# A gather kernel on one Trainium2 core: each gather waits for the landing of the fourth gather ahead of it

## The chip, the cores and the metric

The kernel runs on one core of a Trainium2 chip. A core has a matrix engine (PE, with its weight loads shown as PEld), a vector engine (DVE), a scalar engine (ACT), GpSimd (POOL) and SyncE (SP), each with its own queue of instructions that it works off in order, and 16 DMA engines that they share. The metric is the device time of one execution in microseconds (us); lower is better. Every time comes from the runs or from one profiled execution.

## The reference

Two parts are added to the input `x` (2048 rows of 448), both fed by its layer norm `xn`. The first is a long convolution per channel. The second, a mixture of 4096 experts, is where the change lies: for each row and each of 16 heads, two experts are chosen, their rows of `u` and `v` are fetched, and their outputs are summed. In the code below, `k_shift` is a causal convolution of `k` with four taps, `y` one of `kv` with `ssm_k` over the whole length, done with an FFT; `top_s` and `top_e` are the two best of the four sums made from the two best of `s1` and of `s2`.

```python
def _A_ref(q, k, v, shift_k, ssm_k, ssm_D):
    ...
    kv = k_shift * v
    ...
    return q * (y + kv * ssm_D)

def _B_ref(x, w_q, k1, k2, u, v):
    q = jnp.einsum("nd,dhc->nhc", xf, w_q)
    s1 = jnp.einsum("nhd,ed->nhe", q[..., :dk], k1)
    s2 = jnp.einsum("nhd,ed->nhe", q[..., dk:], k2)
    ...
    g = _softmax(top_s, axis=-1)
    ue = u[top_e]
    ve = v[top_e]
    act = _gelu(jnp.einsum("nd,nhkd->nhk", xf, ue))
    return jnp.einsum("nhk,nhk,nhkd->nd", g, act, ve)

xn = _layernorm(x, axis=-1)
return x + _A_ref(xn, A_k, A_v, A_shift_k, A_ssm_k, A_ssm_D) + _B_ref(xn, B_w_q, B_k1, B_k2, B_u, B_v)
```

## The kernel before

The 2048 rows are 16 tiles (`T`) of 128. For each tile there are 128 x 32 chosen experts, and they are worked on in blocks (`b`, 128 in all, eight per tile). A block is four gathers: one indirect DMA of POOL (L494) takes 128 indices from `idx` and fetches 128 rows of `uv`, the expert's `u` and `v` side by side, 896 float32 each. The four gathers of a block fill one buffer `uv`, and there are four buffers (`NBUF`, the pool `gp`), so POOL can be at most four blocks ahead of the reader that frees a buffer.

A block is then read as follows. `e_spread` (L506) spreads the normed rows into `xr` on PE. `e_dots` multiplies the `u` halves by `xr` on DVE: L525 takes the first `na` of the four gathers in one instruction and leaves their sums to ACT (L544), and L532 takes each of the rest with its sum. ACT applies gelu (L548), DVE weighs by the gate (L559), the weights are spread into `cc`, and PE (L584 and L587) multiplies the `v` halves by `cc` into `pv`. That last matmul frees the buffer: in the code it is the key `("v", b)`, for which the first gather of block b + 4 waits.

The convolution runs in two halves (`g`) beside this, in the second half of the time. `c_load` (L624) brings seven blocks of its inputs from `hkv` with SP's DMAs into `x1`, shown in the profile as `x`; `c_delta` (L660) and `c_prod` on DVE read them first. `c_fm` (L697) brings the tables `fm`, 66 of 128 KB, for its matmuls.

The order of all engines is fixed before the program runs. Each stage is a generator of operations with an assumed cost; a planner (`Planner`) starts them one by one on a model of the engines and writes the instructions out in that order. Waits on the chip come from the dependences between instructions: the tile framework adds semaphore waits where an instruction reads or overwrites what another makes. DMAs of POOL take eight semaphores (`DMASW0` to `DMASW7`) in turn.

Of the kernel before, what the change touches and what calls it, by code (L numbers as in the profile page):

```python
# [185 lines left out]
def parallel_kernel(ctx, tc, x, wq, kk, uv, hkv, const, fq, out):  # L186
    nc = tc.nc
    ctx.enter_context(tc.manual_schedule())
    ap = ctx.enter_context(tc.tile_pool(name="ap", bufs=1))
# [21 lines left out]
    idx = ap.tile([P, NT, NG], I32, name="idx")  # L211
# [14 lines left out]
    live = {}  # L226
# [258 lines left out]
    NB = len(order)  # L485
    HALF = CH * GC

    def e_gather():
        for b, (T, j, hf) in enumerate(order):
            for c in range(4):  # L490
                def go(b=b, T=T, g=8 * j + 4 * hf + c, c=c):
                    if c == 0:
                        live["uv", b] = gp.tile([P, 4, 2 * D], F32, tag="uv", name="uv")
                    nc.gpsimd.indirect_dma_start(live["uv", b][:, c, :], None, uv, bass.IndirectOffsetOnAxis(ap=idx[:, T, g:g + 1], axis=0))  # L494
                yield Op("POOL", 1.25, go, [("idx", T)], key=("land", b, c), moved=4.6e5, rings=[(r_uv, ("v", b))] if c == 0 else [])

    def e_spread():
# [310 lines left out]
    plan.add(2, norm(6, NT))  # L808
    plan.show("weights")
    experts = [plan.add(PRIO.get(s.__name__, 0.0), s()) for s in (e_gather, e_values, e_weigh, e_scale, e_spread, e_dots, e_gelu, e_out, e_fold)]  # L810
    stores = [plan.add(1, e_store(g)) for g in range(2)]
    plan.run(early)
# [72 lines left out]
```

## Time and profile before

| | |
|---|---|
| runs | 998.83, 1013.42 and 1013.01 us, median 1013.01 |
| profiled execution | 1002.79 us |
| its span, first to last instruction | 1001.0 us |
| granted PE clock, mean | 0.853 of full speed |
| DMA | 278.52 MB, mean 278 GB/s over the span |

A group's row in the profile gives line, engine, operation, `output<-inputs`, the form and the count, then busy time in us, mean ns of one, and the idle time of the engine just before these instructions with what ended it. "issue" is waiting for which the profile shows no cause. A wait for several semaphores is put down to the one that came last. In a timeline, each row has start, duration and, in brackets, the idle time before it and who ended that.

### The profile page before, as it was taken

The page shows a single profiled execution, that of the slowest core. Times are in us where ns is not written, and L with a number is a line of the kernel's source. Part 1 is how long each engine was busy: PE and PEld are TensorE (multiplying, and loading weights), DVE is VectorE, ACT ScalarE, POOL GpSimd, SP SyncE. Part 2 cuts the span into 40 slices and gives each one's busy share as a digit, 9 for nine tenths or more (in the row PEclk, how much of TensorE's full clock was granted, in tenths as well). Part 3 has the DMA queues.
Part 4 walks back from the last instruction along what each step waited for, and adds up shares of the span by engine and source line. Part 5 has one row for each costly group of instructions (what it writes and reads, how often), then busy time and mean ns, then how long its engine had stood idle before and what let it go on. Part 6 is the DMA issues. An engine that isn't in the chain of part 4 may idle for free.

```text
span 1001.0 us, 16542 instructions
## 1 busy us (share of the span) xinstructions
PE 741.3 (74%) x5052; PEld 422.7 (42%) x5052; DVE 711.1 (71%) x2621; ACT 543.6 (54%) x1886; POOL 491.5 (49%) x518
## 2 busy tenths in 40 slices
PE   6971889697988878765576777776767665778775
PEld 3550446454454545333443333444444422333443
DVE  3575989698887778773677768873666857789444
ACT  4313786366756566464565546563276554556532
POOL 0024463556655455655465455554355655555450
PEclk9995789898999788865779889997887897899777
DMA  9936785778887787889988688989788878899674
GB/s 343 381 117 234 246 287 192 267 252 300 297 278 267 252 280 251 297 275 378 330 283 266 235 309 274 351 286 381 255 286 277 288 257 295 308 311 329 239 231 148
DMA packets 80553, 278.52 MB, mean 278 GB/s; under 512 B 10320, under 2 KB 47568, under 8 KB 80464
## 3 DMA queue, kind: packets, MB, share of 16 engines
q0 software_dynamic: 40960, 234.91, 67.9%
q1 hardware_dynamic: 39360, 42.41, 12.6%
q8 instruction: 41, 0.67, 0.3%
q10 hardware_dynamic: 144, 0.13, 0.1%
q14 instruction: 48, 0.39, 0.1%
HBM read 273.75 MB, written 3.67 MB: 277 GB/s over the span
## 4 chain that ended last, share of the span: by engine, by line
PE 39%; DVE 23%; issue 11%; ACT 9%; another core or an unknown queue 8%; DMA 7%; POOL 2%; DVEq 0%; SPq 0%; POOLq 0%; ACTq 0%
DVE uv L525 8%; PE pv L587 7%; ACT uv L544 5%; DVE mi L397 5%; PE ps L677 4%; PE psf L705 4%; PE fin L773 4%; DVE mx L399 3%; DMA x<-in_hkv_dram 3%; PE pw L296 3%; PE psu L737 3%; DMA uv<-in_uv_dram,idx 3%; PE sc L355 2%; POOL uv L494 2%
## 5 line engine op out<-in xcount | busy, mean ns | idle before, releaser
L494 POOL DMA_INDIRECT uv<-in_uv_dram,idx x512 | 490.8, 959 | 485.5 <-issue 154.1
L544 ACT ACTIVATE uv<-uv 128x448 f32<-128x448 f32 x459 | 258.9, 568 | 63.4 <-DVE uv L525 38.9
L525 DVE TENSOR_TENSOR uv<-xr,uv 128x1792 f32<-128x1792 f32 (+3 forms) x128 | 233.0, 1822 | 33.4 <-remote 10.4
L587 PE MATMUL pv<-uv,cc 128*32 128x448 f32 x1024 | 154.9, 637 | 0.2 <-issue 0.2
L677 PE MATMUL ps<-cst,x 128*64 128x132 f32 x896 | 80.4, 336 | 45.0 <-issue 16.9
L397 DVE FIND_INDEX8 mi<-mx,sc 128x8 uint32<-128x64 f32 x512 | 104.3, 221 | 6.3 <-issue 6.2
L705 PE MATMUL psf<-x,fm 128*128 128x448 f32 x132 | 74.1, 656 | 36.4 <-DVE hh L728 18.2
L677 PEld LDWEIGHTS ps<-cst,x 128*64 128x64 f32 x896 | 63.9, 168 | 78.7 <-issue 36.8
L399 DVE MAX8 mx<-sc 128x8 f32<-128x64 f32 x512 | 74.1, 214 | 31.1 <-remote 15.8
L355 PE MATMUL sc<-wh,xh 128*128 128x512 f32 x192 | 86.1, 448 | 8.2 <-remote 3.7
L544 ACT ACTIVATION_READ_ACCUMULATOR uv<-uv 128x1 f32 x459 | 87.8, 191 | 0.0
L357 PE MATMUL sc<-wh,xl 128*128 128x512 f32 x192 | 79.4, 413 | 1.1 <-issue 1.1
L356 PE MATMUL sc<-wl,xh 128*128 128x512 f32 x192 | 79.7, 415 | 0.3 <-issue 0.3
L737 PE MATMUL psu<-hh,fm 128*128 128x224 f32 x264 | 67.2, 385 | 16.4 <-remote 5.9
L737 PEld LDWEIGHTS psu<-hh,fm 128*128 128x128 f32 x264 | 52.8, 207 | 47.6 <-issue 30.3
L687 ACT ACTIVATE x<-ps 128x396 f32<-128x396 f32 (+1 forms) x84 | 37.3, 459 | 54.0 <-PE ps L677 35.0
L773 PE MATMUL fin<-cst,zt 128*64 128x64 f32 x896 | 49.5, 259 | 22.5 <-issue 22.0
L574 ACT ACTIVATE cc<-rep,w 128x32 f32<-128x32 f32 x212 | 50.2, 311 | 27.3 <-DVE w L559 17.5
L713 ACT ACTIVATE hh<-psf 128x224 f32<-128x224 f32 x66 | 23.2, 354 | 72.2 <-remote 29.8
L355 PEld LDWEIGHTS sc<-wh,xh 128*128 128x128 f32 x192 | 39.4, 205 | 44.2 <-issue 21.3
L584 PE MATMUL pv<-uv,cc 128*1 128x4 bf16 x128 | 21.6, 169 | 49.3 <-ACT cc L574 19.1
L559 DVE TENSOR_TENSOR w<-ge,gt 128x4 f32<-128x4 f32 x128 | 19.9, 156 | 52.1 <-ACT ge L548 35.1
(98 smaller groups left out, 1057.1 us busy)
## 6 DMA issues: line engine op xcount, KB each, us to landing
wq<-in_wq_dram SPq DMA_DIRECT2D x16, 896.0 KB
x<-in_hkv_dram SPq DMA_DIRECT2D x14, 780.0 KB
fm<-in_fq_dram SPq DMA_DIRECT2D x66, 128.0 KB
uv<-in_uv_dram,idx POOLq DMA_INDIRECT x512
out_dram<-acc SPq DMA_DIRECT2D x32, 112.0 KB
acc<-in_x_dram SPq DMA_DIRECT2D x1, 2240.0 KB
acc<-in_x_dram SPq DMA_DIRECT2D x1, 896.0 KB
cst<-in_const_dram SPq DMA_DIRECT2D x1, 540.0 KB
```

The source lines that it names most:

```text
L355: nc.tensor.matmul(sc, xh[:, c, :], wh[:, c, ns], start=(c == 0), stop=False)
L356: nc.tensor.matmul(sc, xh[:, c, :], wl[:, c, ns], start=False, stop=False)
L397: nc.vector.max_index(mi[:, T % 2, 8 * n + j, :], m, sc[:, 64 * j:64 * j + 64])
L399: nc.vector.max(m, sc[:, 64 * j:64 * j + 64])
L494: nc.gpsimd.indirect_dma_start(live["uv", b][:, c, :], None, uv, bass.IndirectOffsetOnAxis(ap=idx[:, T, g:g + 1], axis=0))
L525: nc.vector.tensor_mul(u, live["xr", T, j][:, None, :D].broadcast_to([P, na, D]), u)
L544: nc.scalar.activation(u, u, AF.Copy, accum_out=live["act", b][:, c:c + 1])
L587: nc.tensor.matmul(pv[32 * c:32 * c + 32, :D], cc[:, c, :], buf[:, c, D:], start=(hf == 0), stop=(hf == 1), tile_position=(0, 32 * c))
L677: nc.tensor.matmul(ps[64 * i:64 * i + 64, w * j:w * j + w], src, f1[:, i, :], start=True, stop=True, tile_position=(0, 64 * i))
L705: nc.tensor.matmul(ps[:, :2 * HALF], live["fm", g, q][:, 0], x1[:, :, :, q, :].rearrange("p c t k -> p t c k"), start=True, stop=True)
L737: nc.tensor.matmul(ps[:, :HALF], fm[:, 1], hh[:, i], start=(i == 0), stop=(i == 1))
L773: nc.tensor.matmul(o[64 * n:64 * n + 64], zt[:, j, 64 * ri:64 * ri + 64], f3[:, ri, n, :], start=(ri == 0), stop=(ri == 1), tile_position= ...
```

## The change

The list `sent` keeps every gather's instruction. From the fifth on, a gather gets a synchronising dependence on the gather four before it in the list, that is, on the same place `c` of the block before. Nothing else in the kernel is altered, and the planner doesn't know of the added dependence, so its order is that of before.

```diff
+    sent = []
+
     def e_gather():
         for b, (T, j, hf) in enumerate(order):
             for c in range(4):
                 def go(b=b, T=T, g=8 * j + 4 * hf + c, c=c):
                     if c == 0:
                         live["uv", b] = gp.tile([P, 4, 2 * D], F32, tag="uv", name="uv")
-                    nc.gpsimd.indirect_dma_start(live["uv", b][:, c, :], None, uv, bass.IndirectOffsetOnAxis(ap=idx[:, T, g:g + 1], axis=0))
+                    made = nc.gpsimd.indirect_dma_start(live["uv", b][:, c, :], None, uv, bass.IndirectOffsetOnAxis(ap=idx[:, T, g:g + 1], axis=0)).ins
+
+                    sent.append(made)
+                    if len(sent) > 4:
+                        tc.add_manual_dep(made, sent[-5].name, mybir.DependencyInfo(mybir.DependencyClass.Sync, mybir.DependencyReason.DATA), reason="pace")
```

On POOL, from the first gather on, the instructions before stand as follows. `DMAHW` are the semaphores of loads by SP or ACT, `DMASW` those of the gathers; the n-th gather raises number n - 1 modulo 8 when it has landed.

```order
L494 DMA uv<-in_uv_dram,idx 128x896 [waits DMAHW3_49,DMAHW2_49,Activation_49]
L494 DMA uv<-in_uv_dram,idx 128x896 x3
L494 DMA uv<-in_uv_dram,idx 128x896 [waits DMAHW5_49,DMAHW4_49,PE_49]
L494 DMA uv<-in_uv_dram,idx 128x896 x3
L494 DMA uv<-in_uv_dram,idx 128x896 [waits DMAHW6_49,DMAHW7_49,DMASW0_49,PE_49]
L494 DMA uv<-in_uv_dram,idx 128x896 [waits DMASW1_49]
L494 DMA uv<-in_uv_dram,idx 128x896 [waits DMASW2_49]
L494 DMA uv<-in_uv_dram,idx 128x896 [waits DMASW3_49]
L494 DMA uv<-in_uv_dram,idx 128x896 [waits DMAHW0_49,DMAHW1_49,DMASW4_49,PE_49]
```

There the first wait on `DMASW0` is the ninth gather's, so a gather waits for the eighth ahead of it. With the change, on the same engine from the same place:

```order
L496 DMA uv<-in_uv_dram,idx 128x896 [waits DMAHW3_49,DMAHW2_49,Activation_49]
L496 DMA uv<-in_uv_dram,idx 128x896 x3
L496 DMA uv<-in_uv_dram,idx 128x896 [waits DMAHW4_49,DMAHW5_49,DMASW0_49,PE_49]
L496 DMA uv<-in_uv_dram,idx 128x896 [waits DMASW1_49]
L496 DMA uv<-in_uv_dram,idx 128x896 [waits DMASW2_49]
L496 DMA uv<-in_uv_dram,idx 128x896 [waits DMASW3_49]
L496 DMA uv<-in_uv_dram,idx 128x896 [waits DMAHW6_49,DMAHW7_49,DMASW4_49,PE_49]
```

Now the fifth gather waits on `DMASW0`, the first gather's, and the ninth on `DMASW4`, the fifth's. The gathers themselves stand in the same places.

## The prediction

> **What bounds the kernel now.** The first view is the page's list of engines, with the group of the gathers and that of their first reader.
>
> ```profile
> PE 741.3 (74%) x5052; PEld 422.7 (42%) x5052; DVE 711.1 (71%) x2621; ACT 543.6 (54%) x1886; POOL 491.5 (49%) x518
> ...
> q0 software_dynamic: 40960, 234.91, 67.9%
> ...
> PE 39%; DVE 23%; issue 11%; ACT 9%; another core or an unknown queue 8%; DMA 7%; POOL 2%; DVEq 0%; SPq 0%; POOLq 0%; ACTq 0%
> ...
> L494 POOL DMA_INDIRECT uv<-in_uv_dram,idx x512 | 490.8, 959 | 485.5 <-issue 154.1
> ...
> L525 DVE TENSOR_TENSOR uv<-xr,uv 128x1792 f32<-128x1792 f32 (+3 forms) x128 | 233.0, 1822 | 33.4 <-remote 10.4
> ```
>
> No engine is full. In the chain that ended last (the row of shares), PE and DVE hold 62% and POOL 2%. POOL is idle for 485.5 us, and since it does nothing in the span but the 512 gathers, that is the time it already spends waiting. They are the queue q0 (packets, MB, share of the 16 DMA engines): one gather is 234.91 MB / 512 = 459 kB. What POOL waits for, and who waits for the gathers, stands in the list of waits:
>
> ```profile
> POOL uv L494 <- issue: 154.1, 393, 9.3
> ...
> POOL uv L494 <- ACT uv L544: 54.0, 17, 8.3
> ...
> POOL uv L494 <- PE pv L587: 44.3, 18, 5.5
> ...
> DVE x L660 <- DMA x<-in_hkv_dram: 12.8, 3, 8.0
> ...
> DVE uv L525 <- DMA uv<-in_uv_dram,idx: 7.0, 7, 3.9
> ...
> PE pv L584 <- DMA uv<-in_uv_dram,idx: 2.6, 1, 2.6
> ...
> ACT uv L544 <- DMA uv<-in_uv_dram,idx: 2.1, 1, 2.1
> ```
>
> The columns are total us, times, longest. POOL's waits are for buffers: PE (L587) is a buffer's last reader. The other way round, an engine waited for a gather's landing 9 times, 11.7 us in all. So the gathers run ahead of their readers nearly everywhere, and the readers set the pace. The pace is on POOL's timeline:
>
> ```profile
> 66.48 1.10 POOL L494 DMA_INDIRECT uv<-in_uv_dram,idx  x1 [65.17 <-ACT gt L462]
> ...
> 71.63 0.94 POOL L494 DMA_INDIRECT uv<-in_uv_dram,idx  x1 [0.30 <-issue]
> 72.88 0.95 POOL L494 DMA_INDIRECT uv<-in_uv_dram,idx  x1 [0.30 <-issue]
> ...
> 307.98 0.95 POOL L494 DMA_INDIRECT uv<-in_uv_dram,idx  x1 [0.30 <-issue]
> 313.20 0.94 POOL L494 DMA_INDIRECT uv<-in_uv_dram,idx  x1 [4.28 <-PE pv L587]
> ...
> 972.99 0.95 POOL L494 DMA_INDIRECT uv<-in_uv_dram,idx  x1 [0.30 <-issue]
> ...
> 976.74 0.95 POOL L494 DMA_INDIRECT uv<-in_uv_dram,idx  x1 [0.30 <-issue]
> ```
>
> Inside a buffer's four gathers one starts every 1.25 us (71.63 to 72.88). Over the run it is (976.74 - 66.48) / 511 = 1.78 us, because the first gather of a buffer usually stands still until the buffer is free (4.28 us at 313.20). Only 33 of the 127 later buffers start with no such pause; the first of those is the row at 71.63, the last that at 972.99.
>
> **The change, part by part.** It adds no instruction and moves none. Each gather from the fifth on gets a wait on the landing of the gather four ahead. In the order of POOL nearly every gather already waits on one of eight DMA semaphores, that of the gather eight ahead; the names of the waits stay and only the gather that is meant moves, from eight ahead to four. The first four waits are new: fifth to eighth gather.
>
> What is one such wait worth? It needs the time from a gather's start to its landing. The chain in order of time shows that whole where a reader did wait:
>
> ```profile
> 128.12 4.81 DMA uv<-in_uv_dram,idx
> ...
> 257.17 5.80 DMA uv<-in_uv_dram,idx
> ...
> 513.37 4.44 DMA uv<-in_uv_dram,idx
> ...
> 591.13 4.83 DMA uv<-in_uv_dram,idx
> ...
> 910.22 6.25 DMA uv<-in_uv_dram,idx
> ```
>
> 4.44 to 6.25 us, mean 5.23. The gather four ahead started 4 x 1.25 = 5.0 us earlier if nothing paused, and over 6 us earlier if the buffer's first gather paused by 1.3 us or more. POOL then needs a moment from release to start. A PE release bounds it:
>
> ```profile
> 311.39 1.54 PE L587 MATMUL pv<-uv,cc 128*32 128x448 f32 x8
> ```
>
> The matmul ends at 311.39 + 1.54 = 312.93 and the gather starts at 313.20: 0.27 us. Could a release by a landing take longer? The nearest row is this one, of the same engine, so I take 0.27; zero is the lower end.
>
> So the new wait costs nothing behind a pause: 5.23 + 0.27 = 5.50 us have gone by already. In an unbroken run it costs 5.50 - 5.00 = 0.50 us (none by the shortest landing, 6.25 + 0.27 - 5.00 = 1.52 by the longest), once per run, since the three gathers after it follow landings that are themselves about a gather apart. With 33 unbroken starts that is 33 x 0.50 = 17 us more of waiting on POOL, at most 33 x 1.52 = 50, set against 485.5 us of idle time.
>
> Of that the end sees little. Behind the waiting gather stand only later gathers, for POOL has no other work, and behind those the readers at L525. What hides the delay is the lead of the landings over the readers; if it goes, DVE is late, then ACT (L544) and PE (L587), then the buffer's release. The 9 exposed waits are where there is no lead. A share of 33 / 127 of them, 2.3, follows an unbroken start: 2.3 x 0.50 = 1.2 us. Were all nine hit at the longest landing, it would be 9 x 1.52 = 13.7 us. Below nothing it can go too: a gather that stands back leaves the DMA engines to the loads of L624, for which DVE waited 12.8 us (row above), so -12.8 us is that end. Between -12.8 and +13.7 I take +1, by the exposed waits, since they are the rows of the very thing that is delayed.
>
> The Trainium skill (DMA: Bandwidth & Descriptors, section Anatomy of one DMA — SWDGE (gpsimd) path) gives one DMA from GpSimd about 2.0 us plus its bytes at 436 GB/s, which for 459 kB is an estimated 3.05 us. By that the wait would never bind, 3.05 being under 5.0, and the sum would be 0 instead of +1. The trace disagrees, with 4.44 to 6.25 us under this kernel's load.
>
> **The sum.** The profiled execution took 1002.8 us (span 1001.0); +1 gives 1004. It stands 1% below the median of the three runs shown, 1013.0, whose lowest is 998.8 and highest 1013.4. I put the forecast between the two, at 1007: the change moves nothing by as much as the runs differ among themselves.
>
> **The rivals.**
>
> *The four-deep loop becomes the bound (slower).* With four in flight a gather can start no oftener than every (landing + release) / 4. At 5.50 us that is 1.38 us, and 1.78 is needed, so there is room. It decides from 4 x 1.78 = 7.1 us on; each 0.1 us above then costs 512 x 0.1 / 4 = 12.8 us. For it speaks the 6.25 row, that landings could lengthen where the loads of L624 compete (below), and that a release by a landing is nowhere shown on POOL. Against it: four of the five landings are under 6, and fewer gathers in flight are no reason for one to land later. At 7.3 us it gives 1003 + 26 = 1029 us. A stage alone doesn't reach it: it must hold through the run.
>
> *The loads of L624 come through sooner (faster).* At 449 us seven loads of 0.8 MB start, beside the gathers, and the chain in order of time waits for the third of them:
>
> ```profile
> 449.17 28.77 DMA x<-in_hkv_dram
> ```
>
> The DMA queues in the window from 453 to 466 us:
>
> ```profile
> q0 software_dynamic: 734, 4.24, 81.9%
> q1 hardware_dynamic: 1083, 0.83, 20.4%
> ```
>
> And from 476 to 484 us, where no gather runs:
>
> ```profile
> q1 hardware_dynamic: 3464, 2.66, 110.6%
> ```
>
> Beside gathers the loads (q1) get 0.83 MB in 13 us, 64 GB/s; alone, 2.66 MB in 8 us, 332 GB/s. A gather queue that runs dry would hand that time over. A pace of 1.38 instead of 1.25 us frees a tenth of q0's 4.24 MB, 0.42 MB, or 0.42 / 0.332 = 1.3 us. If it took away all of DVE's wait it would be 12.8 us: 990. Only if gathers stood aside altogether would the third load land after 3 x 0.8 / 0.332 = 7.2 us instead of 28.77, 21.6 us sooner: 981. Against it: with four in flight the queue hardly empties, four gathers at 1.25 us being 5.0 us of a cycle of 5.50.
>
> The Trainium skill (the same page, section Queues, rings and completion order) has each DMA engine take turns between the queues it has work for, a packet at a time, which is a mechanism for this rival. By it the loads gain only while the gathers' queue is empty; the trace agrees, with 64 GB/s against 332.
>
> *The wait does nothing at all.* If the landings were always done four gathers later, or the eight-deep wait already held POOL to four, the time would be 1003 by the profiled run. Against it stands the 6.25 row, longer than 5.0.
>
> **How the numbers follow.** The forecast (binds in the unbroken runs, absorbed) has 0.70 and the wait that does nothing 0.12. The loads' rival has 0.10, of which 0.04 goes past -2%, the end near 981. The slower rival has 0.08, of which 0.07 is past +2%. A difference of under about 2% can't be told from none in this kernel, whose own runs lie 1.5% apart. So faster 0.04, same 0.89, slower 0.07. The range goes from 993 (near 990, where DVE's whole wait for loads is gone) to 1022 (1007 + 13.7, a little over): both bounds of the sum, and the spread of the runs, lie inside or at its edge; the far ends of both rivals stay outside.
>
> **What would show it right or wrong.** In the changed kernel POOL's spacing inside unbroken runs should go from 1.25 to a mean of 1.3 to 1.5 us (the gather at the place of 71.63 near 72.1), its idle time within some tens of us of 485, now ended by other gathers' landings at more of the starts; the 9 exposed waits for gathers should stay near 12 us, and DVE's wait at L660 near 13. Wrong would be exposed waits of 30 us or more, or a spacing near 1.8 us inside runs (the slower rival), or the chain's 28.77 us of load under 20 (the faster one).

## The result: faster on the first chip, slower on another

On the chip of the prediction the changed kernel took 969.02 us (median of 4 runs, 964.69 to 975.48) against 1013.21 us: a ratio of 0.966, with a 95% interval from 0.959 to 0.973. It is 3.4% faster, and below the range of 993 to 1022.

That is half of the result. The time of the kernel before differs by the chip, or by the moment: 1013 us on the first, 995 on one of the later ones, and 844.6 to 845.5 in six other sets of runs. On such a chip of 845 us the same change, run again, took 899.61 us against 844.58, a ratio of 1.066 (1.063 to 1.070): slower. So there are two questions: why it gained on the first chip, and why it lost on the other.

| | before, first chip | after, first chip | before, 845 us chip | after, 845 us chip |
|---|---|---|---|---|
| profiled execution, us | 1002.79 | 975.48 | 846.59 | 899.89 |
| its span, us | 1001.0 | 973.7 | 844.8 | 898.1 |
| granted PE clock | 0.853 | 0.861 | 0.916 | 0.887 |
| mean time from gather to gather, us | 1.78 | 1.73 | 1.49 | 1.59 |

The last row is (start of the last gather less start of the first) / 511. The lower clock is not a mark of the first chip: a kernel of 1037.4 us span on one of the 845 us chips (the third gather ahead, below) had 0.853 too.

The page of the changed kernel on the first chip: the engines, the chain that ended last, and the groups of the gathers and of their first reader. From L494 on, line numbers are higher than before (L494 is L496, and L525 to L782 are higher by 6).

```profile
PE 738.4 (76%) x5052; PEld 421.8 (43%) x5052; DVE 711.1 (73%) x2621; ACT 544.8 (56%) x1886; POOL 492.0 (51%) x518
...
PE 26%; DVE 23%; DMA 13%; issue 11%; ACT 9%; another core or an unknown queue 6%; POOL 5%; SPq 1%; DVEq 0%; POOLq 0%; ACTq 0%
...
L496 POOL DMA_INDIRECT uv<-in_uv_dram,idx x512 | 491.3, 960 | 458.4 <-issue 125.9
...
L531 DVE TENSOR_TENSOR uv<-xr,uv 128x1792 f32<-128x1792 f32 (+3 forms) x128 | 233.2, 1823 | 38.2 <-DMA uv<-in_uv_dram,idx 21.6
```

Its list of waits (total us, times, longest):

```profile
POOL uv L496 <- DMA uv<-in_uv_dram,idx: 47.1, 54, 2.5
...
DVE uv L531 <- DMA uv<-in_uv_dram,idx: 21.6, 18, 6.1
...
DVE x L666 <- DMA x<-in_hkv_dram: 18.3, 6, 5.6
```

The wait does what it says, with 47.1 us on POOL, and the readers wait longer than before for gathers (21.6 us against 7.0) and for the loads of the convolution (18.3 against 12.8). All of this should make the kernel slower. In the chain, DMA's share goes from 7% to 13%; PE's share falls from 39% to 26%, and "another core or an unknown queue" from 8% to 6%. On one core there is no other core. What these entries are shows best at one place. The timeline of the kernel before, around its gathers from 813 us on (POOL, then ACT, DVE and PE):

```profile
813.11 0.94 POOL L494 DMA_INDIRECT uv<-in_uv_dram,idx  x1 [5.77 <-issue]
...
826.85 0.95 POOL L494 DMA_INDIRECT uv<-in_uv_dram,idx  x1 [0.30 <-issue]
...
831.15 0.94 POOL L494 DMA_INDIRECT uv<-in_uv_dram,idx  x1 [3.36 <-ACT x L745]
...
821.18 0.20 ACT L548 ACTIVATE ge<-act 128x4 f32<-128x4 f32 x1
828.09 0.36 ACT L713 ACTIVATE hh<-psf 128x224 f32<-128x224 f32 x1 [6.71 <-remote]
...
822.58 0.29 DVE L564 TENSOR_TENSOR cc<-rep,w 128x128 f32<-128x128 f32 x1
830.25 1.56 DVE L525 TENSOR_TENSOR uv<-xr,uv 128x1344 f32<-128x1344 f32 x1 [7.37 <-remote]
...
818.00 0.93 PE L705 MATMUL psf<-x,fm 128*128 128x448 f32 x2
...
819.92 1.02 PE L506 MATMUL xr<-xn,rep 32*128 32x448 f32 x4 [0.23 <-issue]
...
823.32 0.95 PE L587 MATMUL pv<-uv,cc 128*32 128x448 f32 x8
```

Twelve gathers run 1.25 us apart, until 827.80. ACT stands still from 821.38 to 828.09, and DVE from 822.87 to 830.25. When the waits that the program gives these two instructions are set against the ends of what they wait for, all of it was over when the instruction ahead of them on their own engine ended: the `psf` that ACT reads at 818.93, the `xr` that DVE reads at 820.94. PE's last instruction of the stretch ended at 824.27. But the trace has the updates of PE's semaphore that let the two go at 828.07 and 830.22. They start late by 6.71 and 7.37 us, 0.3 and 2.5 us after the stretch of gathers has ended. "remote" is how the profile shows such a wait: the update that ended it has no instruction close before it that the profile could name. The largest such rows of the kernel before:

```profile
ACT zt L760 <- remote: 50.0, 11, 6.7
ACT hh L713 <- remote: 29.8, 7, 10.0
ACT idx L461 <- remote: 27.8, 5, 7.6
...
DVE fin L782 <- remote: 22.7, 5, 6.3
```

And the same four of the changed kernel:

```profile
ACT zt L766 <- remote: 44.4, 11, 6.4
ACT idx L461 <- remote: 29.7, 5, 7.0
...
ACT hh L719 <- remote: 4.6, 2, 2.9
...
DVE fin L788 <- remote: 17.4, 5, 5.7
```

All rows of this kind on DVE, ACT and PE come to 204.4 us in 52 waits before and 133.2 us in 40 after (the whole idle time of each, so the most that lateness can be in it). Of the 52, 48 end with an update of PE's semaphore, and of the 40, 39; so it is nearly always PE's result that is told late. In the chain that ended last, the pieces of "an unknown queue" are 7.6% of 1001.0 us before and 5.6% of 973.7 us after, 76 and 55 us: 21 of the 27 us by which the span fell. Stretches of eight or more gathers, each at most 1.6 us behind the last, were 25 before and are one after. Of the 52 late starts 51 end inside a stretch or within 3 us behind it, but only 24 at one of eight or more and 27 at one of four or fewer: short stretches have them too. This is the start of theory S: on that chip, signals between engines come late while POOL issues gathers without a break, and the wait helps by breaking the stretches. At this point it was argued from two traces only.

Those two traces also lack records. 645 DMAs with 16 updates each make 10320 updates by landings; the traces of the first chip hold 5078 of them before and 5319 after, those of the 845 us chip 10236 and 10289. Where the update that ended a wait is missing, the profile puts the wait down to "issue" or to another engine, so the rows of waits of the first chip are lower ends. On POOL of the changed kernel, 53 pauses of more than the usual 0.3 us stand under "issue", 35.1 us in all, beside the 47.1 us. Missing records and late starts come together (5728 and 6552 of 10320 in the two profiles of the chip of 995 us), and every run here has a span and a clock, so was recorded: whether the recording itself has a part in the late starts is not shown, and no run here tests it.

### The profile page after: what moved, and what is told of

Its sections match the earlier page's. It is cut to its first block, busy times and chain, and to the rows that moved or that the text cites. A ratio compares the mean times of both kernels' runs of the same rounds, so it can differ in the third digit from the quotient of the medians.

```text
span 973.7 us, 16544 instructions
## 1 busy us (share of the span) xinstructions
PE 738.4 (76%) x5052; PEld 421.8 (43%) x5052; DVE 711.1 (73%) x2621; ACT 544.8 (56%) x1886; POOL 492.0 (51%) x518
## 2 busy tenths in 40 slices
DMA packets 80553, 278.52 MB, mean 286 GB/s; under 512 B 10320, under 2 KB 47568, under 8 KB 80464
## 4 chain that ended last, share of the span: by engine, by line
PE 26%; DVE 23%; DMA 13%; issue 11%; ACT 9%; another core or an unknown queue 6%; POOL 5%; SPq 1%; DVEq 0%; POOLq 0%; ACTq 0%
DMA uv<-in_uv_dram,idx 11%; DVE uv L531 9%; ACT uv L550 5%; PE pv L593 5%; POOL uv L496 5%; DVE mi L397 4%; PE fin L779 3%; PE ps L683 3%; DVE mx L399 3%; DMA x<-in_hkv_dram 2%; PE sc L355 2%; PE sc L356 2%; PE sc L357 2%; PE psf L711 1%
## 5 line engine op out<-in xcount | busy, mean ns | idle before, releaser
L496 POOL DMA_INDIRECT uv<-in_uv_dram,idx x512 | 491.3, 960 | 458.4 <-issue 125.9
L531 DVE TENSOR_TENSOR uv<-xr,uv 128x1792 f32<-128x1792 f32 (+3 forms) x128 | 233.2, 1823 | 38.2 <-DMA uv<-in_uv_dram,idx 21.6
L593 PE MATMUL pv<-uv,cc 128*32 128x448 f32 x1024 | 160.8, 652 | 0.2 <-ACT uv L550 0.2
L711 PE MATMUL psf<-x,fm 128*128 128x448 f32 x132 | 71.3, 630 | 30.9 <-DVE hh L734 10.1
L590 PE MATMUL pv<-uv,cc 128*1 128x4 bf16 x128 | 21.6, 169 | 68.9 <-DVE cc L570 24.8
L590 PEld LDWEIGHTS <-cc 128*1 128x1 bf16 x128 | 10.3, 80 | 122.3 <-issue 40.4
L779 PE MATMUL fin<-cst,zt 128*64 128x64 f32 x896 | 46.7, 258 | 19.4 <-issue 18.8
```

The lines of the kernel that those rows point to most:

```text
L496: made = nc.gpsimd.indirect_dma_start(live["uv", b][:, c, :], None, uv, bass.IndirectOffsetOnAxis(ap=idx[:, T, g:g + 1], axis=0)).ins
L531: nc.vector.tensor_mul(u, live["xr", T, j][:, None, :D].broadcast_to([P, na, D]), u)
L593: nc.tensor.matmul(pv[32 * c:32 * c + 32, :D], cc[:, c, :], buf[:, c, D:], start=(hf == 0), stop=(hf == 1), tile_position=(0, 32 * c))
L711: nc.tensor.matmul(ps[:, :2 * HALF], live["fm", g, q][:, 0], x1[:, :, :, q, :].rearrange("p c t k -> p t c k"), start=True, stop=True)
```

## The experiments

The texts on record name theories by letters. S: breaks in POOL's stretches of gathers let late signals through. Q, later F: with fewer gathers in flight the loads of the other queue come sooner. B: only the beginning matters, where 16 gathers run ahead. C: the sign depends on whether the chip shows late signals. L: the loop of landing, release and next issue is the price of the wait. "A chip of late signals" is one on which the kernel before takes 995 or 1013 us and its trace has rows with "remote".

### Pauses, fewer waits, a deeper wait, a wait at the beginning only

Four kernels on one chip, where the kernel before took 844.91 us. First, no wait, but four memsets of a 128x128 tile on POOL ahead of each buffer's first gather:

```diff
                     if c == 0:
+                        if b:
+                            for _ in range(4):
+                                nc.gpsimd.memset(idle, 0.0)
                         live["uv", b] = gp.tile([P, 4, 2 * D], F32, tag="uv", name="uv")
```

> The kernel before, with four small memsets (128x128, some 1.2 us together) on POOL ahead of each buffer's first gather, and no added wait for landings. Theory S (while POOL issues gathers without a break, signals between the other engines arrive late; any break lets them through): about 0.97 of the time before, no more than 0.98, and the waits that end 1 to 2 us after a run of 8 or more gathers are gone. Rival Q (what helps is that never more than four gathers are in flight): 0.97 to 1.00, since a break of 1.2 us lets about one gather land and so caps most runs too. Rival B (the gain comes from the first 16 gathers alone): about 0.99.

Second, the wait on the first gather of a buffer alone:

```diff
-                    if len(sent) > 4:
+                    if c == 0 and len(sent) > 4:
```

> The changed kernel with the added wait on the first gather of each buffer only; the other three keep the wait on the eighth gather ahead. S: the same as the changed kernel, 0.96 to 0.975, since one short break per four gathers is left. Q: between, 0.97 to 0.99, for five can again be in flight. B: 0.99.

Third, the wait on the fifth gather ahead:

```diff
-                    if len(sent) > 4:
-                        tc.add_manual_dep(made, sent[-5].name, ...
+                    if len(sent) > 5:
+                        tc.add_manual_dep(made, sent[-6].name, ...
```

> Each gather waits for the landing of the fifth ahead. The landings took about 5.3 us and the fifth ahead started 6.25 us earlier in an unbroken run, so the wait seldom binds and runs of 8 stay whole. S: 0.99 to 1.00, most of the gain is lost. Q: before had five others in flight at only 9 of 512 gathers, so also 0.99 to 1.00. A general gain from fewer outstanding gathers without a threshold would leave some 0.975 to 0.985.

Fourth, the wait on gathers 5 to 16 only:

```diff
-                    if len(sent) > 4:
+                    if 4 < len(sent) <= 16:
```

> The added wait on the 5th to the 16th gather only. The first DVE multiply stood at 87.4 us before and 77.3 us after, and 6.4 us of that lead were left at the eighth buffer. B: 0.965 to 0.975. S and Q: that lead alone, 6 us or 0.994, so 0.99 to 1.00.

| kernel | us | ratio to before | 95% interval | gather to gather, us |
|---|---|---|---|---|
| pauses | 924.57 | 1.096 | 1.090 to 1.101 | 1.64 |
| wait on a buffer's first gather | 889.90 | 1.053 | 1.047 to 1.060 | 1.58 |
| fifth ahead | 841.24 | 0.997 | 0.993 to 1.000 | 1.48 |
| gathers 5 to 16 | 845.15 | 0.999 | 0.996 to 1.003 | 1.49 |

Nothing gained here, and whatever held POOL back cost some per cent. The fifth ahead is harmless where the fourth is not, so the price is not that of a wait as such. B falls for this kind of chip: a wait at the beginning alone changes nothing. Since the traces of these four runs have no row "remote", they say nothing about the first chip. Before going on, the two kernels of the case had to be seen on a chip of this kind.

### Both kernels again, and the signals by themselves

A small kernel measures a signal's way by itself and computes nothing of the reference: DVE, PE and ACT hand a tile round 250 times while POOL issues 24 gathers without a break, then 24 with the fourth-ahead wait, then 24 with memsets between fours.

```diff
+    for h in range(HOPS):
+        marks[h] = nc.vector.tensor_copy(a, b).ins
+        nc.tensor.matmul(pt[:, :8], ident, a, start=True, stop=True)
+        nc.scalar.activation(b, pt[:, :8], AF.Copy)
...
+    unbroken()
+    paced()
+    paused()
```

> A kernel that computes nothing of the reference: DVE, PE and ACT pass a 128x8 tile round by signals, 250 times, while POOL issues 24 gathers of 128x896 without a break, then 24 with the wait on the fourth ahead, then 24 with four memsets of 128x128 ahead of every fourth. S: on a chip where signals come late, the round takes several us longer from about the fifth unbroken gather until 1 to 2 us behind the last, and stays even in the second and third part; on a chip where they don't (as in the runs e1 to e4, with 845 us for the kernel before), it is even in all three. If late signals had nothing to do with gathers, the long rounds would be strewn over the whole kernel.

> The changed kernel once more. Theory C (the gain depends on the chip: the wait breaks up runs of gathers, which pays only where signals come late in them; where they don't, the wait only slows the gathers): 0.96 to 0.975 beside a kernel before of about 1010 us, and 1.01 to 1.05 beside one of about 845, there because four in flight give one gather every (5.4 + 0.3) / 4 = 1.42 us and the kernel before uses (840 - 90) / 511 = 1.47 on average, with no spare for the stretches that need more. Rival (the gain is the change's own on any chip): 0.96 to 0.975 beside either.

> The kernel before, for its profile on the chip of e5 and e6. C: where it takes about 845 us, POOL's unbroken runs are longer than 16 in places and no wait ends on its own 1 to 2 us behind them; where it takes about 1010 us, runs of 8 end in such waits, as in the profile shown ahead of the prediction.

The kernel before took 844.58 us on this chip, the changed one 899.61: 1.066 (1.063 to 1.070). The page of the kernel before there (the gathers' queue, chain by engine, the gathers), and two of its waits:

```profile
q0 software_dynamic: 40960, 234.91, 76.1%
...
DVE 47%; PE 21%; DMA 15%; ACT 5%; issue 5%; SPq 4%; POOL 2%; DVEq 0%; POOLq 0%; ACTq 0%
...
L494 POOL DMA_INDIRECT uv<-in_uv_dram,idx x512 | 493.7, 964 | 331.3 <-issue 145.5
```

```profile
POOL uv L494 <- DMA uv<-in_uv_dram,idx: 4.9, 16, 0.3
...
DVE uv L525 <- DMA uv<-in_uv_dram,idx: 26.8, 16, 6.4
```

The changed kernel there:

```profile
L496 POOL DMA_INDIRECT uv<-in_uv_dram,idx x512 | 491.8, 961 | 388.3 <-DMA uv<-in_uv_dram,idx 118.1
```

```profile
POOL uv L496 <- DMA uv<-in_uv_dram,idx: 118.1, 160, 2.4
...
DVE uv L531 <- DMA uv<-in_uv_dram,idx: 85.0, 60, 7.7
```

Here the chain of the kernel before has no "unknown queue" at all, where it had 8% on the first chip, and no engine has a wait with "remote". Without late starts the readers want a gather every 1.49 us, not every 1.78, and POOL's idle time is 331.3 us, not 485.5. The wait now bites: POOL waits 118.1 us for landings, and DVE waits 85.0 us for gathers, 58 us more than before, which is about the 53 us by which the span grew (898.1 less 844.8). Slower transfers explain little of the 156 us between the two spans: the gathers' packets took 76.1% of 844.8 us here and 67.9% of 1001.0 us there, 643 and 680 us.

PE itself differs too. In the program, the 16 matmuls of one operation of `c_fin` (L773) wait for nothing between them. First the kernel before on the first chip, where POOL issues gathers every 1.25 us from 686.20 to 695.89, then on the 845 us chip, inside a stretch of twelve gathers:

```profile
690.41 0.35 PE L773 MATMUL fin<-cst,zt 128*64 128x64 f32 x5 [0.77 <-issue]
691.86 0.34 PE L773 MATMUL fin<-cst,zt 128*64 128x64 f32 x4 [1.11 <-issue]
693.30 0.49 PE L773 MATMUL fin<-cst,zt 128*64 128x64 f32 x4 [1.10 <-issue]
```

```profile
581.26 2.08 PE L773 MATMUL fin<-cst,zt 128*64 128x64 f32 x64
```

The 16 matmuls that begin at 690.41 took 4.84 us; on the 845 us chip no operation of 16 took more than 1.12 us. On the first chip 9 of the 56 operations took over 2 us before and 8 after. So "late signals" is too narrow a name: beside gathers PE's own instructions too come late there. What the two have in common stays open.

In the small kernel ACT's rounds (start, duration, idle before), first ahead of the gathers and then in the unbroken piece:

```profile
31.91 0.18 ACT L37 ACTIVATE b<-pt 128x8 f32<-128x8 f32 x1 [0.89 <-PE pt L36]
32.97 0.18 ACT L37 ACTIVATE b<-pt 128x8 f32<-128x8 f32 x1 [0.89 <-PE pt L36]
...
47.92 0.18 ACT L37 ACTIVATE b<-pt 128x8 f32<-128x8 f32 x1 [1.07 <-PE pt L36]
49.17 0.18 ACT L37 ACTIVATE b<-pt 128x8 f32<-128x8 f32 x1 [1.08 <-PE pt L36]
```

A round is 1.07 us without gathers and 1.25 us beside them, the very spacing of the gathers, and no round in its four runs took more than 1.31 us. Signals are touched by unbroken gathers even here, by 0.2 us a round and not by several us.

### The third gather ahead

```diff
-                    if len(sent) > 4:
-                        tc.add_manual_dep(made, sent[-5].name, ...
+                    if len(sent) > 3:
+                        tc.add_manual_dep(made, sent[-4].name, ...
```

> The same wait, for the third gather ahead instead of the fourth. Theory L (the loop of landing, release and issue is the price): on a chip where the kernel before takes some 845 us, a gather comes every (5.4 + 0.3) / 3 = 1.9 us at best where the fourth-ahead wait allowed 1.43, and the 0.14 us that each gather lost above the loop there makes 2.04 us; 512 gathers then take some 1045 us, a ratio of 1.15 to 1.25 against the kernel before. Theory C (the sign depends on whether signals between the engines come late): on a chip where the kernel before takes some 1010 us and its multiplies have time to spare, the stretches of unbroken gathers are cut shorter still, but the loop now allows only one gather per 1.9 us where 1.78 are needed: ratio 1.00 to 1.06, that is, worse than the 0.966 of the fourth-ahead wait. If the price were only the extra instruction or semaphore of each wait (rival), the ratio stays at that of the fourth-ahead wait: 1.066 on the one chip, 0.966 on the other.

Measured: 1040.79 us against 844.83, ratio 1.233 (1.227 to 1.239). The page (chain by engine, gathers, their median from issue to landing), and two waits:

```profile
DMA 56%; DVE 19%; PE 11%; issue 8%; POOL 4%; ACT 2%; DVEq 0%; POOLq 0%; SPq 0%; ACTq 0%
...
L496 POOL DMA_INDIRECT uv<-in_uv_dram,idx x512 | 490.0, 957 | 529.4 <-DMA uv<-in_uv_dram,idx 235.3
...
uv<-in_uv_dram,idx POOLq DMA_INDIRECT x512, 4.9
```

```profile
DVE uv L531 <- DMA uv<-in_uv_dram,idx: 218.7, 112, 11.1
...
POOL uv L496 <- DMA uv<-in_uv_dram,idx: 235.3, 229, 5.2
```

The loop is now the bound: more than half of the chain is gathers. A gather comes every 1.87 us, a little oftener than the 2.04 expected, since with three in flight it lands in 4.9 us where it took a median of 5.9 us in the kernel before and 5.4 with four, on the other chip of 845 us: (4.9 + 0.3) / 3 + 0.14 = 1.87, with the 0.3 us of release and the 0.14 us of the expectation. So L holds, in order of depth: the fifth ahead 0.997, the fourth 1.066, the third 1.233. The rival, a fixed price for each wait, is out. The Trainium skill (DMA: Bandwidth & Descriptors, section Anatomy of one DMA — SWDGE (gpsimd) path) would have a gather land in an estimated 3.05 us; with fewer in flight the traces come nearer to that and don't reach it (the shortest with three is 4.0 us).

The pauses and the small kernel ran on the same chip.

> Four small memsets on GpSimd ahead of each buffer's first gather, no wait on landings. Theory C: where the kernel before takes some 1010 us and its trace shows instructions that start microseconds after the last thing they waited for, the memsets break the stretches of gathers as the wait does, so the ratio is 0.96 to 0.98 there; where it takes some 845 us and no instruction starts late, it is 1.09 to 1.10 as measured before. The rival (the gain on the first chip comes from fewer gathers in flight, not from breaks in GpSimd's stretches): 1.00 or above in both.

> VectorE, TensorE and ScalarE hand a tile round 250 times while GpSimd issues 24 gathers without a break, then with the fourth-ahead wait, then with memsets between fours; nothing of the reference is computed. Theory C: on a chip where the kernel before takes some 1010 us, rounds inside the unbroken piece take 3 to 9 us, those in the two other pieces under 2; where it takes some 845 us, all take 1.0 to 1.35 us as measured before. Rival: rounds of 1.0 to 1.35 us in all pieces on either chip, and the late starts of the whole kernel have another cause.

The pauses came to 1.095 (1.089 to 1.100), as before, and no round of the small kernel was late. This chip too was one without late signals.

### Slow the readers down, then add the wait

If L is right, the wait costs nothing where gathers are wanted seldom enough, as on the first chip. Five multiplies of a 128x128 tile with itself, which feed nothing, go ahead of each buffer's own multiplies on DVE. First without the wait, then with it:

```diff
             def begin(b=b):
                 live["act", b] = rp.tile([P, 4], F32, tag="act", name="act")
+                for _ in range(5):
+                    nc.vector.tensor_mul(load, load, load)
```

> No added wait. Five multiplies of a 128x128 tile with itself on VectorE ahead of each buffer's own multiplies, which feed nothing: 128 x 5 x 0.29 us = 188 us more on VectorE. It is the base for the next run: where the kernel before takes some 845 us, VectorE becomes the bound and the kernel takes 950 to 1040 us, with gathers wanted every 1.75 to 1.95 us (the 82 us ahead of the first gather and behind the last taken off, over 512) instead of 1.49. Ratio 1.12 to 1.23; both theories expect the same here.

> The same five multiplies and the wait on the fourth gather ahead. Theory L (the wait costs only where gathers are wanted faster than the loop of four lets them come, 1.57 us each in the changed kernel on such a chip): wanted every 1.75 to 1.95 us, the gathers have time to spare and the wait costs nothing: within 1.5% of the run without it, as my prediction had it for the first chip. Rival (the wait costs a fixed amount per gather, 55 us over 512 on a chip of 845 us): 5 to 6% slower than the run without it. Neither expects it to be faster than the run without it by over 1.5% on a chip whose signals are not late; on a chip where the kernel before takes some 1010 us theory C expects it faster by 2 to 4%.

On a chip where the kernel before took 844.75 us, they took 997.87 us and 989.55 us. The wait, which cost 6.6% without the load, now takes 0.8% off: 989.55 / 997.87 = 0.992, and 0.988 to 0.998 between the furthest runs. Gathers came every 1.79 and 1.77 us. Both lists of waits, the load alone first:

```profile
DVE x L664 <- DMA x<-in_hkv_dram: 25.3, 4, 8.0
...
DVE uv L529 <- DMA uv<-in_uv_dram,idx: 2.7, 5, 1.1
```

```profile
DVE x L670 <- DMA x<-in_hkv_dram: 9.7, 4, 4.7
...
DVE uv L535 <- DMA uv<-in_uv_dram,idx: 6.5, 6, 2.7
```

DVE waits 3.8 us more for gathers and 15.6 us less for the convolution's loads. So L is confirmed from its other side. Theory Q may have a small share, with fewer gathers in flight letting the loads through; that is argued from one trace of each, and the 0.8% is small. It is not what happened on the first chip, where the wait for these loads grew (12.8 to 18.3 us), nor is 0.8% as large as 3.4%.

### Pauses where gathers have spare time, on a chip of late signals

What parts S from F is to break the stretches without holding a gather for a landing: the load on DVE, and eight memsets of 128x16 on POOL ahead of each buffer's first gather.

```diff
+    idle = ap.tile([P, 16], F32, name="idle")
...
                     if c == 0:
+                        if b:
+                            for _ in range(8):
+                                nc.gpsimd.memset(idle, 0.0)
```

> The five extra multiplies on VectorE, no wait, and eight memsets of 128x16 on GpSimd ahead of each buffer's first gather (1.0 to 1.2 us by the rows of memsets before): they break GpSimd's stretches as the wait does, without holding a gather back for a landing. Theory F (what the wait gains under the extra load comes from fewer gathers in flight, so that the loads of the other queue land sooner): no gain here, 0.995 to 1.02 of the run with the load alone. Theory S (it comes from breaking the stretches of gathers): 0.985 to 0.995 of it on a chip whose signals are not late, and 0.95 to 0.98 where the kernel before takes some 1010 us.

> The five extra multiplies on VectorE alone, as a base on the same chip: 993 to 1001 us and a ratio of 1.175 to 1.19 where the kernel before takes some 845 us. Where it takes some 1010 us: 1120 to 1200 us, with instructions in the trace that start microseconds after the last thing they waited for.

These two fell on a chip where the kernel before took 994.8 us. The load alone took 1065.68 us, which is less than the 1120 to 1200 expected, and the load with pauses 1012.14: 0.950, from 0.943 to 0.956 between the furthest runs. Late starts of ACT and the wait for the convolution's loads in the list of waits, of the load alone and then of the load with pauses:

```profile
ACT zt L764 <- remote: 42.8, 11, 6.1
...
ACT hh L717 <- remote: 21.5, 7, 6.5
...
DVE x L664 <- DMA x<-in_hkv_dram: 11.4, 2, 5.8
```

```profile
ACT zt L768 <- remote: 31.6, 10, 5.7
...
DVE x L668 <- DMA x<-in_hkv_dram: 10.9, 3, 4.6
```

All "remote" rows on DVE, ACT and PE fall from 117.9 us in 37 waits to 61.4 us in 25; the row of `hh`, 21.5 us, is gone, while that of DVE's `fin` did not fall (14.6 and 19.1 us). The span fell by 53.1 us (1066.8 to 1013.7). The wait for the convolution's loads, on which F rests, moved by half a us. Breaks in POOL's stretches give time back on such a chip without any wait for a landing. 37 of the 37 late starts without the pauses end inside a stretch of gathers or within 3 us behind it, and so do all 25 with them, now at stretches of at most four: the pauses make them fewer and shorter, and don't end them.

### The control, and what was not met again

Two more sets of runs were to place the small kernel, and pauses without the load, on a chip of late signals, and to try load and pauses on one without.

> The hand-round of VectorE, TensorE and ScalarE beside GpSimd's gathers once more (nothing of the reference is computed), for the case that it falls on a chip of late signals. Where the kernel before takes some 995 to 1013 us, theory S has rounds of 3 to 9 us in the unbroken piece and under 2 us in the two others; where it takes some 845 us all rounds take 1.0 to 1.35 us as measured before. Rival on a chip of late signals (the lateness belongs to many engines' and queues' traffic together, not to GpSimd's gathers alone): 1.0 to 1.35 us in all pieces there too.

> The four memsets on GpSimd ahead of each buffer, no wait, no extra load. Theory S: 0.95 to 0.98 of the kernel before where that takes some 995 to 1013 us, 1.09 to 1.10 where it takes some 845 us. Rival (the extra load made the gain of the pauses on the chip of late signals): 1.00 to 1.10 on either.

> The five extra multiplies on VectorE and the pauses of GpSimd, now as a control: on a chip where the kernel before takes some 845 us there are no late signals for the pauses to cure, so theory S has 0.99 to 1.03 of the 998 us that the load alone took there (ratio to the kernel before 1.17 to 1.21), against the 0.95 measured on the chip of late signals. Rival (the pauses gain by something that has to do with the load, on any chip): 0.95 here too, ratio 1.11 to 1.14.

> The hand-round beside gathers again (nothing of the reference is computed). Where the kernel before takes some 995 to 1013 us, theory S has rounds of 3 to 9 us in the unbroken piece and under 2 us in the two others; where it takes some 845 us all take 1.0 to 1.35 us. Rival on a chip of late signals: 1.0 to 1.35 us there too, and the lateness needs the whole kernel's traffic.

Both sets fell on chips of 845 us. Pauses alone: 1.095 (1.090 to 1.101), a third time. Load and pauses: 993.08 us, or 1.179 (1.170 to 1.187) of the kernel before, against 1.182 (1.175 to 1.188) for the load alone on another such chip: no difference that can be told. So load and pauses make four cells:

| | load alone | load and pauses |
|---|---|---|
| chip without late signals | 997.87 us | 993.08 us |
| chip with late signals | 1065.68 us | 1012.14 us |

The gain of 5% belongs to the chip and not to the load. The small kernel took 278.56 to 279.77 us in its four runs, and its rounds never were late; it did not meet a chip of late signals. Whether POOL's gathers alone make signals late, or only beside the whole kernel's traffic, stays open. The changed kernel itself, and pauses without the load, were not run on the second chip of late signals either.

## Why the prediction was wrong

- **The wait on POOL: right in kind, low in size.** The fifth gather was not held; the sixth started 0.50 us late, as costed. POOL's timeline of the changed kernel on the first chip:

```profile
70.59 0.94 POOL L496 DMA_INDIRECT uv<-in_uv_dram,idx  x1 [0.30 <-issue]
72.33 0.94 POOL L496 DMA_INDIRECT uv<-in_uv_dram,idx  x1 [0.80 <-issue]
...
79.43 0.94 POOL L496 DMA_INDIRECT uv<-in_uv_dram,idx  x1 [0.67 <-DMA uv<-in_uv_dram,idx]
```

  From 70.59 to 79.43 are six spacings of 1.47 us, inside the 1.3 to 1.5 predicted. POOL's idle time came to 458.4 us, within tens of 485. But the new waits were to cost 17 us, at most 50, and 47.1 us are on record as a lower end: the gathers wait oftener than once per unbroken run (54 times, and up to 53 more under "issue"). The change also adds two instructions where the prediction had none (16544 against 16542 in the profile); nothing hangs on them.
- **The exposed waits for gathers: the direction right, the size not.** They were to stay near 12 us, with +1.2 for the change. The changed kernel has 21.6 us at L531, where it was 7.0. Rows of PE come to 8.3 us more, but at lines that read no gather (L344, L711, L612), so their cause is uncertain; with them it is 30 in all, +18. The 11.7 us that the prediction began from came from a trace with half of the landings' updates missing, so they are a lower end as well.
- **The loads of L624: the bound didn't come.** DVE's wait for them grew from 12.8 to 18.3 us. The chain's longest piece of load fell from 28.77 to 20.41 us, not under the 20 that I had named.
- **The step that failed** is the lower end of the sum: "Below nothing it can go too", with -12.8 us from the loads as "that end". I had quoted 8% "another core or an unknown queue" and "remote 10.4" on L525 and given them no term, so the time that the change gave back stood in no row of the sum. In the runs it was those pieces that fell, from 76 to 55 us in the chain, and from 204.4 to 133.2 us over all rows. The bound should have been those 8%, some 76 us of a chain of 1001. The chance of 0.04 for a gain followed from that. "The readers set the pace" held, but what set theirs was in part these late starts, not work. The trace of before already showed that a change to POOL's rhythm might reach them: the row at 828.09 stands right behind the end of a stretch of gathers.
- **The slower rival was right for a chip of 845 us.** "The four-deep loop becomes the bound" was priced for a gather each 1.78 us, from a landing of 7.1 us on. At 1.49 us the point is 4 x 1.49 = 5.96 us, and landing with release is 5.4 + 0.3 = 5.7 us in the median: no margin. The mechanism was right, and the run with the third ahead showed it pure; the pace that I set against it was the first chip's, slowed by late starts.

Shown: the loop's price by depth and by pace; that pauses, beside the load, gain on a chip of late signals and not on others. Argued from traces: that the changed kernel's gain on the first chip is the same thing, by its 71 us fewer of "remote" and its broken stretches. Open: what makes PE's signals and PE's own instructions late beside gathers, whether the recording has a part in it, and whether it belongs to the chip or to the moment.

## What to carry to other kernels

A share of the chain that the profile can't name ("remote", "unknown queue") is a term of the sum: look what its waits end with, and take its whole size as the bound of a gain. A cap on transfers in flight costs nothing as long as (landing + release) / depth stays well under the time in which the readers want the next, and its price rises steeply from there; so set the depth by the fastest pace that the kernel has anywhere (here five, tried on a chip of 845 us alone), not by that of a slow profile. And a ratio of a few per cent that was measured on one chip is to be seen on a second one before it is kept.

## What the runs showed of the hardware that was not expected

- The same kernel took 1013, 995 or 845 us, by the chip or the moment. On the first two, instructions on ACT, DVE and PE started up to 9.2 us after what they waited for had ended (ACT's at 595.16 of the first trace, for matmuls that ended by 585.98); 48 of 52 such waits there ended with an update of PE's semaphore; on the others no wait was put down to "remote".
- On the first of them 16 matmuls with nothing to wait for between them took up to 6.38 us beside gathers; on the 845 us chip 1.12 us at most.
- In the four traces of those two chips 37% to 51% of the updates by landings are missing (5078 to 6552 of 10320 are there); in the two kernels' traces on the 845 us chip under 1%.
- On the chips of 1013 and 995 us these late starts become fewer when POOL's stretches of gathers are broken, by a wait (204.4 to 133.2 us) or by memsets (117.9 to 61.4 us).
- On a chip of 845 us a round of signals through three engines takes 1.07 us alone and 1.25 us, the gathers' own spacing, beside unbroken gathers.
- A gather's landing gets shorter with fewer in flight, on chips of 845 us: a median of 5.9 us without the wait, 5.4 with four and 4.9 with three.
